# Stages one and four of a Fourier mixing in 64 x 64 quarters of the array, from even and odd sums

## The chip, the cores and the metric

The kernel runs on one core of a Trainium2 chip. The metric is the device time of one launch in microseconds (us), the median of several runs. TensorE (PE) multiplies matrices, VectorE (DVE) and ScalarE (ACT) do elementwise work and copy results out of PSUM, the memory that products are written to, POOL (GpSimd) issues the indirect DMAs and some sums, and SyncE (SP) issues all other DMAs. All arrays are float32.

## The reference

Two blocks follow one another. The first filters along the sequence in the frequency domain, the second sends each token through one of eight experts.

```python
batch, seq, dim = (8, 2496, 256)
X = np.fft.rfft(x, axis=1)
y = np.fft.irfft(X * (filt_r + 1j * filt_i)[None], n=seq, axis=1)

x = y.reshape(19968, 256)                       # N, D
logits = x @ w_gate                             # D x 8
expert_idx = np.argmax(logits, axis=1)
probs = softmax(logits); gate_w = probs[np.arange(N), expert_idx]
for e in range(8):                              # tokens of expert e
    h = np.maximum(x_sorted[lo:hi] @ w1[e], 0)  # 256 x 1024
    y_sorted[lo:hi] = h @ w2[e]                 # 1024 x 256
out = gate_w[:, None] * y_sorted[inv_perm]
```

## The kernel before

*The transform.* The sequence length is 2496 = 39 x 64. By the Chinese remainder theorem a token has two indices: q modulo 39 (`N1`) and t modulo 64 (`N2`). Each batch goes through four stages of products. Stage one (`stage_a`) is a real transform along q: 39 reals become 20 cosine and 20 sine sums. Three values of t (`NB`) share one product, with a block-diagonal table `tas` of 117 x 120. Stage two (`stage_b`, table `tbs`) is the complex transform along t, and the filter `ht` is multiplied in on VectorE. Stage three (`stage_c`, `tcs`) goes back along t, and stage four (`stage_d`, `tds`, 120 x 117) back along q.

The input of stage one is laid out on the host (`lay_x`) as 128 rows of 22 groups (`NG`), of which 117 rows are used; the last group has one t and not three. Stages one and four work in six chunks a batch, five of four groups and one of two (`CH`). Two groups are one product of 512 columns (2 x 256 channels), and each product gets a bank of PSUM (`bank`, seven of them) and one copy out of it (`evac`), on VectorE or ScalarE, whichever the planner holds to be free sooner. Between the stages the data go through memory and come back with another index on the rows: `zo` is stored to `zd` and loaded as z (`by_part`), `uo` is stored to `ud` and loaded as u (`columns`). All loads land in one set of seven buffers, `fin` (`NIN`). The first batch (`first_a`, `first_c`) stays on the chip.

*The routing.* Behind stage four each chunk `yo` is turned (`turn_y`; from batch 3 on in blocks of 32 on VectorE), multiplied with the gate (`block_logits`: eight products of 32 output columns each) and routed (`route`): small operations on VectorE find the expert and the place of each row, and one indirect DMA per group (`scatter`) writes the rows with their token number (`ids0`) and gate to `rowsd` in memory, in the order of the experts. From batch 3 on, all 128 rows of a group take part with a mask (`vld`).

*The experts.* Tiles of 512, 256 or 128 rows are read back (`rows_in`), multiplied with `w1` (`hidden_by_quarters`: both matrices in four blocks, seven products of blocks where the definition has eight, with sums on POOL and VectorE) and with `w2` (`result`, or, once the transform is done and its memory is free, `result_by_quarters`, again seven for eight).

*What sets the order.* A planner (`Order`) writes the order of each engine's instructions by hand while the program is built. It keeps a clock for each engine, with a price for each operation, and knows when a tile is ready. `slot(k)` lists the steps of the transform for batch k+1 (stage one), k (two and three) and k-1 (four and routing), each with a place in the slot, a load, its TensorE time and a class; steps of one class keep their order. The main loop takes the first step or expert product that is ready within 0.2 us and doles out products among the steps by a credit (`share`). SyncE's loads are issued by `more_loads`, stores by `flush`. Every instruction is issued by one helper, so all carry line L246 in the profile, and groups are told apart by tile names.

The lines that the change touches most are `stage_a` (530), `stage_d` (580), `columns` (473), `by_part` (503), `load_z` (515), `load_u` (520), `stage_c` (565), `route` (739), `slot` (1217), the tables in `dft_tables` (56) and the layout in `lay_x` (106). The core of stage one is

```python
for j in range(0, n, 2):
    p = bank()
    mm(p[:TK, :], lhsT=tas, rhs=xt[:TP, j:j + 2, :], start=True, stop=True)
    evac(zo[:, j:j + 2, :], p[:TK, :].rearrange("p (t d) -> p t d", t=2), 512)
```

Of the kernel before, what the change touches and what calls it, by code (L numbers as in the profile page):

```python
# [19 lines left out]
P = 128  # L20
S = 2496
# [13 lines left out]
TK = NB * NS  # L35
DH = D // P
# [4 lines left out]
NJ = D // CT  # L41

# [13 lines left out]
def dft_tables():  # L56
# [24 lines left out]

    ids = np.zeros((NB, N1, NG))
    valid = np.zeros((NB, N1, NG))
    for j in range(NB):
# [3 lines left out]

    by_block = np.zeros((4, CT, NG + 2))
    by_block.reshape(P, NG + 2)[:TP, :NG] = valid.reshape(TP, NG)  # L90
# [5 lines left out]
        "ta": ta.reshape(TP, TK),  # L96
        "tb": tb,
        "tc": tc,
        "td": np.pad(td.reshape(TK, TP), ((0, 0), (0, P - TP))),
        "sg": np.concatenate([sg[:, :NF // 2], sg[:, NF // 2:]]),  # L100
        "ids": ids.reshape(TP, NG),
        "valid": np.concatenate([np.pad(valid.reshape(TP, NG), ((0, P - TP), (0, 0))), by_block], axis=1),
    }


def lay_x(x):

    out = np.zeros((x.shape[0], P, NG, D), x.dtype)
    q = np.arange(N1)
    for j in range(NB):  # L110
        for i in range(len(range(j, N2, NB))):
            out[:, j * N1:(j + 1) * N1, i] = x[:, token(q, NB * i + j)]
    return out
# [11 lines left out]
class Order:  # L125
# [53 lines left out]
    def count(self, engine, op, args, named):  # L179
# [31 lines left out]
        else:  # L211
            if out is None:
                took = 0.8 if engine == "sync" else 0.02
            elif engine == "tensor":
# [3 lines left out]
                took = max(0.1, 0.00085 * n) if op == "transpose" else max(0.216, 0.00169 * n) if rows > 32 else 0.00045 * n  # L218
                took *= 2.0 if start < self.slow else 1.0
# [31 lines left out]
class Slots:  # L251
# [3 lines left out]
    def freed(self, name, tag):  # L255

        if name is None:
            return 0.0
        if tag in self.live and name in self.live[tag]():
            return 1e9  # L260
        return max(self.order.done.get(name, 0.0), self.order.used.get(name, 0.0)) + 0.1
# [32 lines left out]
def kernel(  # L294
# [12 lines left out]
    ids: bass.AP,  # L307
    valid: bass.AP,
# [25 lines left out]
    TR = E * TE  # L334

    dram = open_pool(ctx, name="dram", bufs=1, space=DRAM)
    zd = [dram.tile([N2, NS, D], F32, tag=f"z{b % 2}", name="zd") for b in range(B)]
    ud = [dram.tile([N2, NS, D], F32, tag=f"u{b % 2}", name="ud") for b in range(B)]
# [3 lines left out]
    rowsd = dram.tile([TR, DR], F32, tag="rows", name="rows")  # L342
# [18 lines left out]
    tas = cst.tile([TP, TK], F32, name="tas")  # L361
    tbs = cst.tile([P, P], F32, name="tbs")
    tcs = cst.tile([P, P], F32, name="tcs")
    tds = cst.tile([TK, P], F32, name="tds")
# [15 lines left out]
    ids0 = cst.tile([TP, NG], F32, name="ids0")  # L380
    vld = cst.tile([P, 2 * NG + 2], F32, name="vld")
# [12 lines left out]
    ps.live["bank"] = lambda: ()  # L394
# [25 lines left out]
    def load_filters(c):  # L420
        f0, n = FH[c]
        if c == 0:
            nc.sync.dma_start(out=tbs, in_=tb)
# [11 lines left out]
        if c == 0:  # L435
            nc.sync.dma_start(out=tcs, in_=tcm)

    def load_rest():
        nc.sync.dma_start(out=tds, in_=td)
# [33 lines left out]
    def columns(ap, i0, n):  # L473

        rows = ap.rearrange("t s d -> (t s) d")
        m = min(n, NG - 1 - i0)
        yield TK, slice(0, m), rows[i0 * TK:(i0 + m) * TK, :].rearrange("(i p) d -> p i d", p=TK)
        if m < n:
            yield NS, slice(m, n), rows[(NG - 1) * TK:, :].rearrange("(i p) d -> p i d", p=NS)
# [23 lines left out]
    def by_part(ap):  # L503

        return ap.rearrange("t (c f) d -> (t c) f d", c=2)

# [8 lines left out]
    def load_z(b, c):  # L515
        f0, n = FH[c]
        zi = fin(("z", b, c))
        nc.sync.dma_start(out=zi[:, :n], in_=by_part(zd[b])[:, f0:f0 + n, :])

    def load_u(b, c):  # L520
        i0, n = CH[c]
        ui = fin(("u", b, c))
        for r, m, v in columns(ud[b], i0, n):
# [5 lines left out]

    def stage_a(b, c):  # L530
        i0, n = CH[c]
        xt = ins.pop(("x", b, c))
        zo = sb.tile([TK, 4, D], F32, tag="st", name="zo", bufs=4)
        for j in range(0, n, 2):
            p = bank()
            mm(p[:TK, :], lhsT=tas, rhs=xt[:TP, j:j + 2, :], start=True, stop=True)
            evac(zo[:, j:j + 2, :], p[:TK, :].rearrange("p (t d) -> p t d", t=2), 512)
        for r, m, v in columns(zd[b], i0, n):
# [4 lines left out]
    def stage_b(b, f):  # L543
# [6 lines left out]
        mm(p, lhsT=tbs, rhs=zi[:, j:j + 2, :], start=True, stop=True)  # L550
# [14 lines left out]
    def stage_c(b, f):  # L565
# [4 lines left out]
        uo = outs["u", b]  # L570
        p = bank()
        mm(p, lhsT=tcs, rhs=ys, start=True, stop=True)
        evac(uo[:, j:j + 2, :], p.rearrange("p (i d) -> p i d", i=2), 512)
        if j == 2:
            f0 = f - 2
            move(by_part(ud[b])[:, f0:f0 + 4, :], uo)
# [3 lines left out]
    def stage_d(b, c):  # L580
# [7 lines left out]
        yo = outs["o", b, c] = sb.tile([P, 4, DR], F32, tag="y", name="yo", bufs=YB)  # L588
        for j in range(0, n, 2):
            p = bank()  # L590
            if i0 + j + 2 < NG:
                mm(p, lhsT=tds, rhs=ui[:TK, j:j + 2, :], start=True, stop=True)
# [6 lines left out]


# [12 lines left out]
    def first_a(c):  # L613
        i0, n = CH[c]
        xt = ins.pop(("x", 0, c))
        for j in range(0, n, 2):
            p = bank()[:, :4 * TK]
            for h in range(DH):
                for i in range(2):
                    mm(p[:, (2 * h + i) * TK:(2 * h + i + 1) * TK], lhsT=xt[:TP, j + i, h * P:(h + 1) * P], rhs=tas,  # L620
# [21 lines left out]
    def first_c(f):  # L642
        ys = outs.pop(("y", 0, f))
        p = bank().rearrange("p (h i t c) -> p h i t c", h=DH, c=2, i=2)
        for i in range(2):
            for h in range(DH):
                mm(p[:, h, i].rearrange("p t c -> p (t c)"), lhsT=ys[:, i, h * P:(h + 1) * P],
                   rhs=tcs, start=True, stop=True)
# [90 lines left out]
    def route(b, c0, c1):  # L739
# [63 lines left out]
        if by_blocks(b):  # L803
# [13 lines left out]
            nc.vector.tensor_copy(row.rearrange("p (c g) -> p g c", g=4), pr[:, :, 0])  # L817
# [5 lines left out]
        for i, yo in enumerate(yos):  # L823
            n = min(4, w - 4 * i)
            sh8 = (TP, n, 8)
            nc.gpsimd.tensor_scalar(
                yo.bitcast(I32)[:TP, :n, D:D + 8], in0=ids0[:, t0 + 4 * i:t0 + 4 * i + n, None].to_broadcast(sh8),
# [3 lines left out]
        for i in range(w):  # L831
            m = N1 if t0 + i == NG - 1 else TP
# [116 lines left out]
    def rows_in(i):  # L949
# [4 lines left out]
        ng = gis[i] = pools["moe"].tile([P, 4, DR - D], F32, tag="ng", name="ng", bufs=8)  # L954
# [262 lines left out]
    def slot(k):  # L1217
# [12 lines left out]
        elif k < B:  # L1230
            for f in range(0, NF + 4, 2):
                at = f / (NF + 4)
                if f < NF:
                    steps.append((at, lambda f=f: stage_b(k, f), ("z", k, f // 4) if f % 4 == 0 else None, 0.85, "b", lambda f=f: count("y") < 4 and [ins["z", k, f // 4]]))
                if f >= 4:
                    steps.append((at + 0.01, lambda f=f: stage_c(k, f - 4), None, 0.85, "c", lambda f=f: [outs["y", k, f - 4], 0.0 if f % 4 else sb.free("st") - 0.9]))
# [338 lines left out]
```

## Time and profile before

| | |
|---|---|
| median of 3 runs | 1475.87 us (1473.42 to 1477.14) |
| the profiled execution | 1478.19 us, span 1476.5 us |
| TensorE busy | 1440.1 us, 98% |
| its weight loads | 1147.0 us, 78% |
| VectorE busy | 848.7 us, 57% |
| ScalarE busy | 480.6 us, 33% |
| POOL busy | 822.0 us, 56% |
| products with `tas` (stage one, batches 1 to 7) | 154 records, 75.5 us |
| products with `tds` from memory (stage four, batches 1 to 7) | 168 records, 77.1 us |

A product in float32 shows as two records, each with its own weight load. Records overlap, so a group's busy time is what its records cover and not the sum of their durations. Idle time is put down to the instruction that ended it. The stages of the transform lie between the start and about 890 us, where the last logits are computed; the rest is expert products.

### The profile page before, as it was taken

To read this page: it belongs to the slowest core of one execution; us is meant where nothing else is said; L and a number is where in the kernel's file an instruction comes from. 1 tells how busy PE (TensorE), PEld (TensorE's weight loads), DVE (VectorE), ACT (ScalarE), POOL (GpSimd) and SP (SyncE) were. 2 spreads that over 40 slices of the span, in tenths; PEclk is the share of its full clock that TensorE was granted. 3 is DMA by queue.
4 is the path that set the end of the run, shared out by engine and by line. 5 is a ranking of instruction groups with operands and counts; after the bars stand their busy time and mean duration, and the time that the engine had idled before them with its cause. 6 is when DMAs were issued, how large, how long until landed. Compare 5 with 4: busy or idle time off the path is not lost.

```text
span 1476.5 us, 25693 instructions
## 1 busy us (share of the span) xinstructions
PE 1440.1 (98%) x7828; PEld 1147.0 (78%) x7828; DVE 848.7 (57%) x1819; ACT 480.6 (33%) x1004; POOL 822.0 (56%) x1213
## 2 busy tenths in 40 slices
PE   8998998999999999999999999999999999999998
PEld 6543656877677777776787778879999998999997
DVE  4667579235866675457665465567878775431110
ACT  4554452333332232322222232223232322223332
POOL 4434445635555654655465656858989878831111
PEclk9999999999999999999999999999999999999999
DMA  9759889795985585556544735556655425456661
GB/s 269 230 193 340 280 291 299 253 258 185 321 206 167 172 260 151 131 162 229 156 119 132 214 93 148 153 177 188 173 173 167 133 71 137 135 189 176 174 190 43
DMA packets 216383, 278.19 MB, mean 188 GB/s; under 512 B 124131, under 2 KB 163708, under 8 KB 216245
## 3 DMA queue, kind: packets, MB, share of 16 engines
q1 hardware_dynamic: 197125, 233.19, 53.2%
q0 software_dynamic: 19120, 43.33, 8.4%
q8 instruction: 66, 1.08, 0.3%
q14 instruction: 72, 0.59, 0.1%
HBM read 196.45 MB, written 80.64 MB: 188 GB/s over the span
## 4 chain that ended last, share of the span: by engine, by line
PE 85%; DVE 6%; DMA 4%; issue 3%; ACT 1%; POOL 0%; SPq 0%; DVEq 0%; POOLq 0%; ACTq 0%
PE bank L246 83%; DMA fin<-in_x_dram 2%; PE lt L246 2%; DVE hT L246 1%; DVE yw L246 1%; DVE ys L246 1%; DMA fin<-ud 1%; DMA fin<-zd 1%; DMA zd<-zo 1%; POOL out_dram L246 0%; DVE take L246 0%; ACT hT L246 0%; SPq L246 0%; DMA w1t<-in_moe_w_dram 0%; DMA xg<-rows 0%
## 5 line engine op out<-in xcount | busy, mean ns | idle before, releaser
L246 DVE TENSOR_TENSOR hT<-bank,hT 128x512 f32<-128x512 f32 (+1 forms) x504 | 301.9, 626 | 181.4 <-PE bank L246 101.2
L246 PE MATMUL bank<-w2t,hT 128*128 128x256 f32 (+1 forms) x1984 | 388.6, 350 | 1.6 <-DVE hT L246 1.6
L246 PEld LDWEIGHTS bank<-w2t,hT 128*128 128x128 f32 x1984 | 334.5, 190 | 49.9 <-issue 9.6
L246 PE MATMUL bank<-xT,w1t 128*128 128x256 f32 (+1 forms) x1728 | 314.9, 328 | 0.3 <-DVE hT L246 0.3
L246 POOL DMA_INDIRECT out_dram<-ys,ng x161 | 160.0, 994 | 252.5 <-ACT ys L246 121.5
L246 PEld LDWEIGHTS bank<-xT,w1t 128*128 128x128 f32 x1728 | 264.6, 191 | 33.1 <-issue 9.9
L246 ACT ACTIVATE hT<-hT 128x1024 f32<-128x1024 f32 (+1 forms) x144 | 135.5, 960 | 399.8 <-DVE hT L246 387.4
L246 POOL DMA_INDIRECT rows<-yo,row x176 | 181.9, 1033 | 70.8 <-POOL yo L246 31.3
L246 ACT ACTIVATE ys<-bank,ng 128x256 f32<-128x256 f32 x102 | 48.4, 475 | 287.4 <-PE bank L246 231.7
L246 PE MATMUL bank<-sums,wsum 128*128 128x256 f32 (+1 forms) x576 | 135.7, 358 | 1.5 <-DVE hT L246 1.5
L246 PE MATMUL bank<-w2s,hT 128*128 x592 | 132.9, 380 | 1.3 <-ACT hT L246 1.3
L246 POOL TENSOR_TENSOR wsum<-w1t 128x256 f32<-128x256 f32 x72 | 60.1, 835 | 114.5 <-PE bank L246 96.7
L246 PEld LDWEIGHTS bank<-w2s,hT 128*128 128x128 f32 x592 | 110.2, 190 | 15.8 <-ACT hT L246 2.0
L246 PEld LDWEIGHTS bank<-sums,wsum 128*128 128x128 f32 x576 | 100.3, 190 | 21.6 <-issue 11.3
L246 DVE STREAM_TRANSPOSE xT<-xg 128x512 f32<-128x512 f32 (+2 forms) x126 | 57.5, 494 | 57.7 <-PE bank L246 56.9
L246 PE MATMUL bank<-ys,tcs 128*128 128x512 f32 x140 | 73.8, 613 | 7.6 <-DVE yw L246 4.2
L246 DVE TENSOR_TENSOR ys<-bank,ht 128x512 f32<-128x512 f32 x80 | 54.9, 686 | 44.3 <-PE bank L246 38.0
L246 PE MATMUL bank<-fin,tds 120*128 120x512 f32 (+1 forms) x168 | 77.1, 580 | 3.1 <-DMA fin<-ud 2.6
L246 PE MATMUL bank<-fin,tas 117*120 117x512 f32 x154 | 75.5, 608 | 4.2 <-DMA fin<-in_x_dram 3.3
L246 PE MATMUL bank<-fin,tbs 128*128 128x512 f32 x140 | 72.7, 607 | 2.3 <-DMA fin<-zd 2.2
L246 ACT ACTIVATE hT<-bank 128x128 f32<-128x128 f32 (+1 forms) x191 | 57.2, 303 | 53.9 <-PE bank L246 45.3
L246 PE MATMUL bank<-xT,wsum 128*128 128x256 f32 (+1 forms) x288 | 68.8, 362 | 1.1 <-DVE yw L246 0.9
(171 smaller groups left out, 1778.9 us busy)
## 6 DMA issues: line engine op xcount, KB each, us to landing
w1t<-in_moe_w_dram SPq DMA_DIRECT2D x126, 512.0 KB
w2t<-in_moe_w_dram SPq DMA_DIRECT2D x68, 512.0 KB
fin<-in_x_dram SPq DMA_DIRECT2D x39, 512.0 KB
fin<-zd SPq DMA_DIRECT2D x35, 512.0 KB
ud<-uo SPq DMA_DIRECT2D x35, 512.0 KB
fin<-ud SPq DMA_DIRECT2D x35, 512.0 KB
zd<-zo SPq DMA_DIRECT2D x35, 480.0 KB
xg<-rows SPq DMA_DIRECT2D x112, 128.0 KB
```

What stands on the lines that cost most here:

```text
L246: return real(*args, **named)
```

## The change

From batch 4 on (`BA`) stage one, and from batch 3 on (`BD`) stage four, use that a cosine is even and a sine odd in q. The sums x[q] + x[39-q] meet only the cosines, the differences only the sines, each with 20 values of q. With three values of t that is 60 rows and 60 columns, so each product fits a 64 x 64 quarter of the array. A chunk of four groups is now four products of 64 rows, 64 columns and 512 moving columns: even and odd parts for each half of the groups. Two banks take them, so that the two halves of rows write to different banks in stage one, and the even and the odd part in stage four.

- `lay_x` puts q and 39-q into two slots of the same row; `fold_x` makes sum and difference in place, two operations on VectorE for each chunk, one chunk ahead of `stage_a`.
- `stage_d` copies out the odd bank only; `fold_y` adds it to, and subtracts it from, the even bank, two operations on VectorE. The even bank stays taken until then (`count("odd") < 2`).
- The parts lie 64 rows apart in `zd` and `ud`; a group has 128 rows. A load of z or a store of u is then two DMAs, one of 126 rows and one of two. Rows 60 to 63 of each half are unused; `stage_c` fills them in `ud` by two more DMAs a batch.
- The four tables have a second version each, loaded into the same tile during the run (`load_table`): `ta` in slot 3, `tb` and `td` in slot 4, `tc` in slot 3.
- Scatters carry 124 rows (`YR`) where they carried 117; rows with no token go to places behind the table (`waste`, `NW`), and the place is a maximum in the operation that copied it before.
- The planner has prices for these products (0.29 and 0.17 us), two classes "x" and "y" for the folds, and asks for two free banks for chunks of both stages. The buffers of `ng` are 7 and not 8, and the first large tile behind the transform goes by `result_by_quarters` only if its sums were begun.

```diff
+TH = NB * NF
+YR = 64 + TH
+BA, BD = 4, 3
+    taq = np.zeros((2, 64, 2, 64))
+    tdq = np.zeros((2, 64, 64))
+    for f in range(NF):
+        for r, (qr, j) in enumerate(half_rows()):
+            ang = w * ((qr * f) % N1) / N1
+            taq[:, r, 0, j * NF + f] = np.cos(ang)
+            tdq[0, j * NF + f, r] = (2.0 if f else 1.0) / S * np.cos(ang)
+            if f:
+                taq[:, r, 1, j * NF + f] = -np.sin(ang)
+                tdq[1, j * NF + f, r] = -2.0 / S * np.sin(ang)
...
+    def load_table(name, of, k):
+        tables[name] = cst.tile([P, P], F32, tag=name, name=name)
+        nc.sync.dma_start(out=tables[name], in_=of[k])
...
+    def by_part(rows, tile, quarters, f0, n):
+        if not quarters:
+            yield tile[:, :n], rows[:N2 * NS].rearrange("(t c f) d -> (t c) f d", c=2, f=NF)[:, f0:f0 + n, :]
+            return
+        m = 2 * (NG - 1)
+        for lo, hi, r in ((0, m * NB, NB), (m * NB, P, 1)):
+            at = rows[lo // NB * 64 + f0, :]
+            to = tile[lo:hi, :n]
+            dims = [[64 * D, (hi - lo) // r]] + ([[NF * D, r]] if r > 1 else []) + [[1, n * D]]
+            yield bass.AP(to.tensor, to.offset, [list(to.ap[0]), [1, n * D]]), bass.AP(at.tensor, at.offset, dims)
...
+    def fold_x(b, c):
+        m = CH[c][1] // 2
+        xt = ins["x", b, c][:YR]
+        even, odd = xt[:, :m], xt[:, m:2 * m]
+        nc.vector.tensor_tensor(odd, even, odd, op=ALU.subtract)
+        nc.vector.scalar_tensor_tensor(out=even, in0=even, scalar=2.0, in1=odd, op0=ALU.mult, op1=ALU.subtract)
+        folded.add((b, c))
...
+            m = n // 2
+            both = [bank()[:, :m * D].rearrange("p (t d) -> p t d", t=m) for _ in range(2)]
+            for part in range(2):
+                at = slice(64 * part, 64 * part + 64)
+                for h in range(2):
+                    k = slice(64 * h, 64 * h + TH)
+                    mm(both[h][at], lhsT=ta[k, at], rhs=xt[k, part * m:part * m + m], start=True, stop=True)
+            for h in range(2):
+                evac(zo[:, h * m:(h + 1) * m], both[h], m * D)
...
+        if b >= BD and f == 0:
+            at = ud[b][TH, :]
+            nc.sync.dma_start(out=bass.AP(at.tensor, at.offset, [[64 * D, 2 * NG - 2], [1, 4 * D]]), in_=ht[:2 * NG - 2, :4, :].rearrange("p f d -> p (f d)"))
+            nc.sync.dma_start(out=ud[b][(NG - 1) * P:, :], in_=ht[:, 0, :])
...
+        if b >= BD:
+            m = n // 2
+            both = [bank() for _ in range(2)]
+            for h in range(2):
+                for part in range(2):
+                    k = slice(64 * part, 64 * part + TH)
+                    mm(both[part][64 * h:64 * h + 64, :m * D].rearrange("p (i d) -> p i d", i=m), lhsT=tds[k, :64],
+                       rhs=ui[k, h * m:(h + 1) * m, :], start=True, stop=True)
+            evac(yo[:, m:n, :D], both[1][:, :m * D].rearrange("p (i d) -> p i d", i=m), m * D)
+            outs["odd", b, c] = both[0]
+            return
...
+    def fold_y(b, c):
+        m = CH[c][1] // 2
+        even = outs.pop(("odd", b, c))[:, :m * D].rearrange("p (i d) -> p i d", i=m)
+        yo = outs["o", b, c]
+        nc.vector.tensor_tensor(yo[:, :m, :D], even, yo[:, m:2 * m, :D], op=ALU.add)
+        nc.vector.tensor_tensor(yo[:, m:2 * m, :D], even, yo[:, m:2 * m, :D], op=ALU.subtract)
...
-        ng = gis[i] = pools["moe"].tile([P, 4, DR - D], F32, tag="ng", name="ng", bufs=8)
+        ng = gis[i] = pools["moe"].tile([P, 4, DR - D], F32, tag="ng", name="ng", bufs=7)
...
-            if late and i < LARGE:
+            if late and i < LARGE and (wide or i in made):
```

## The prediction

> **What bounds the kernel now.** I read four views in this order: the page's busy times, the table of stretches, the order of time on TensorE around one step of the transform, and the groups of VectorE with the waits of TensorE. Durations below are those of the one profiled execution: its span is 1476.5 us and its own time 1478.19 us; the median of the runs shown is 1475.87 us, 2.3 us below it, so the forecast is the median less the sum found on the profiled execution.
>
> ```profile
> span 1476.5 us, 25693 instructions
> ...
> PE 1440.1 (98%) x7828; PEld 1147.0 (78%) x7828; DVE 848.7 (57%) x1819; ACT 480.6 (33%) x1004; POOL 822.0 (56%) x1213
> ...
> PE 85%; DVE 6%; DMA 4%; issue 3%; ACT 1%; POOL 0%; SPq 0%; DVEq 0%; POOLq 0%; ACTq 0%
> ```
>
> TensorE is busy for 98% of the span and is 85% of the chain that ended last. So the end moves with the time that TensorE needs, as long as nothing else becomes late. The stretches (columns: length, then busy us and instructions of PE, PEld, DVE, ACT, POOL; then clock, DMA share, GB/s) show whether that holds where the change is, some 325 to 890 us, and what comes behind:
>
> ```profile
> 300.00:400.00 100.00, 100.00 (x483) 68.13 (x482) 60.06 (x134) 36.29 (x85) 51.07 (x83) 1.00 0.78 259
> 400.00:500.00 100.00, 98.70 (x502) 76.57 (x502) 61.53 (x123) 28.70 (x54) 55.99 (x87) 1.00 0.64 179
> 500.00:600.00 100.00, 99.29 (x442) 74.20 (x441) 66.89 (x141) 31.32 (x58) 51.52 (x82) 1.00 0.67 202
> 600.00:700.00 100.00, 97.54 (x474) 73.82 (x474) 61.97 (x121) 27.11 (x51) 55.64 (x87) 1.00 0.56 174
> 700.00:800.00 100.00, 100.00 (x511) 78.70 (x511) 63.86 (x135) 30.27 (x57) 53.65 (x83) 1.00 0.47 131
> 800.00:900.00 100.00, 97.19 (x531) 76.06 (x530) 52.68 (x126) 29.78 (x58) 62.39 (x99) 1.00 0.52 156
> 1000.00:1100.00 100.00, 100.00 (x681) 94.03 (x680) 79.16 (x110) 29.01 (x44) 87.44 (x94) 1.00 0.61 179
> ```
>
> From 300 to 900 us TensorE is at 97 to 100% at the full granted clock while VectorE is at 53 to 67% (367 us of 600) and the DMA engines at 47 to 78%. From 1000 to 1100 VectorE is at 79% and TensorE still has no gap: 79% of VectorE is not too much by itself. The third view has both kinds of product that I need (start, length, then records; a product in f32 leaves two records):
>
> ```profile
> 703.48 7.07 PE L246 MATMUL bank<-w2t,hT 128*128 128x256 f32 x32
> 710.48 0.64 PE L246 MATMUL lt<-yt,wb 128*32 128x128 f32 x16
> 711.05 3.72 PE L246 MATMUL bank<-w2t,hT 128*128 128x256 f32 x16
> ...
> 715.69 1.88 PE L246 MATMUL bank<-fin,tds 120*128 120x512 f32 x4
> 717.41 1.89 PE L246 MATMUL bank<-xT,w1t 128*128 128x256 f32 x8
> ```
>
> Two products of stage four (512 columns, whole array) take 717.41 - 715.69 = 1.72 us, 0.43 a record. The eight products with 32 output columns each start within 711.05 - 710.48 = 0.57 us. One after another, their 16 records of 128 columns would take 16 x 0.107 = 1.71 us (0.43 x 128/512 = 0.107), so they ran side by side, four at a time: 0.43 us. The remaining 0.14 us, and the 0.09 us between 703.48 + 32 x 0.2155 = 710.39 and 710.48, are the price of going into and out of the divided array: 0.23 to 0.24 us a visit.
>
> **The change, part by part.**
>
> *Products.* A chunk of four groups in stage one (batches 4 to 7) or four (batches 3 to 7) has two whole-array products, 1.72 us. It becomes four of 64 x 64 with 512 columns, each on its own quarter. If the four run side by side as the four strips did, they take 2 x 0.43 = 0.86 us. There are 4 x 5 + 5 x 5 = 45 such chunks; the nine last chunks of a batch have two groups, 0.86 us before and 0.43 after. Streaming saved: 45 x 0.86 + 9 x 0.43 = 42.6 us. In the changed order the 54 chunks stand in 46 runs (eight pairs adjoin), so 46 x 0.24 = 11.0 us of visits; nine of their borders touch the strip products, which switch anyway, about 0.1 us each back. Net 42.6 - 11.0 + 0.9 = 32.5 us. No row shows quarters (64 rows and 64 columns), so the price is bounded: four at a time saves 32.5 us; one at a time costs 45 x 1.72 + 9 x 0.86 = 85 us plus the visits, +95 us. I take four at a time: the nearest row, the strips, has it.
>
> A rule of the Trainium skill speaks against part of this. Besides the row above, in which four strips over the same 128 rows follow one another without a visible load, "TensorE: Matmul & The Clock Gate", Part 3, says that a weight load overlaps running products only when its row group differs. Two quarters here share each row group, so the second half's loads would stand bare; by that page's load time (its columns over 1.2 GHz, 64/1.2 = 53 ns, an estimate) the sum would be some 54 x 0.1 = 5 us less. I go by the row.
>
> *VectorE.* Added: 24 folds of x, two operations each in SBUF, and 30 folds of the output, two each from PSUM. The nearest rows (count, then busy us and mean ns):
>
> ```profile
> L246 DVE TENSOR_TENSOR hT<-bank,hT 128x512 f32<-128x512 f32 x392 | 257.8, 685 | 138.5 <-PE bank L246 92.6 <-ACT hT L246 30.9 <-issue 1.5
> L246 DVE SCALAR_TENSOR_TENSOR yw<-bank,ht 64x512 f32<-64x512 f32 x80 | 55.4, 693 | 1.1
> L246 DVE TENSOR_TENSOR ys<-ys,yw 128x512 f32<-128x512 f32 x64 | 46.1, 721 | 2.2
> L246 DVE TENSOR_TENSOR hT<-bank,hT 128x256 f32<-128x256 f32 x112 | 44.0, 421 | 42.9 <-ACT hT L246 29.1 <-PE bank L246 8.6
> ```
>
> x: 20 x (0.72 + 0.69) + 8 x 0.42 = 31.6 us. Output: 50 x 0.685 + 10 x 0.42 = 38.5 us. 70 us in all; the copies out of PSUM move a little between VectorE and ScalarE (9 more of stage one on VectorE, 6 fewer of stage four), +2 us, while ScalarE loses half of stage four's copies, about 25. VectorE from 300 on: (367 + 72) over 600 - 33 = 567 us, 77%, under the 79% that TensorE bore without a gap. Cover: the products of the experts' part, which the planner puts between the steps. If it is gone, TensorE waits for a bank or an hT. What TensorE waits for now:
>
> ```profile
> PE bank L246 <- DVE yw L246: 5.1, 3, 3.4
> PE bank L246 <- DVE hT L246: 3.9, 5, 1.6
> PE bank L246 <- DVE ys L246: 3.4, 3, 1.6
> PE bank L246 <- DMA fin<-in_x_dram: 3.3, 2, 2.4
> ```
>
> The three of VectorE are 12.4 us against 849 us of its work; 72 us more in proportion is 1 us, but queues grow faster than load, so I take +4 (bounds 0 and the whole 72). A fold of x also waits for its DMA at the head of VectorE's queue, where hT's additions stand behind it; TensorE waited 3.3 us for these loads in the whole run, so this sits inside the 4. The even bank is held until the fold, one or two banks of seven for about 2 us.
>
> *Tables, queues, rest.* Four tables are loaded a second time into the same tiles. Each load waits on SyncE for the last product that reads the old table, and what is queued behind it (stores, loads of z, u and weights) waits too; the first chunk of the stage then waits some 3 us for landing, which products cover. 0 to 4 x 3 us; I take 2. SyncE issues 51 more DMAs (45 two-row remainders, ten fills of unused rows, tables, less the last groups' separate ones), at some 0.4 us each 20 us over 570, on a queue that stands waiting for TensorE for 445 us of the run: nothing, bounds 0 and 5. Scatters carry 124 rows for 117; POOL is at 51 to 62% there: nothing, bounds 0 and 3. The tile `ng` has 7 buffers for 8: nothing, 0 to 2. One more tile goes through `result_by_quarters` (10 for 9): 112 records of 128 columns at 0.112 for 64 of 256 at 0.216, 12.5 for 13.8 us, -1.
>
> *Sum.* -32.5 - 1 + 4 + 2 = -27.5 us: 1478.19 becomes 1450.7, and on the median 1475.87 - 27.5 = 1448 us.
>
> **Rivals.**
> *A, as above*, 1440 to 1458: the bounds of the small terms, and the few us by which a new order changes small gaps.
> *B, VectorE or a queue takes half of it.* For it: VectorE goes from 61 to 77% where its work is chains of small routing operations and not the regular pattern of 1000 to 1100; a fold sits between the product and the transposition of the output. Against: from 300 to 900 the view of waits for that stretch has TensorE waiting 3.1 us for VectorE's ys, lt, yw and hT parts. If 15 us more of the 72 are bare, 1463; the range is 1458 to 1473.
> *C, slower: the quarters run two at a time.* The strips divide columns alone; no row divides rows. Then a chunk takes 1.72 + 0.24 against 1.72: nothing saved, 46 x 0.24 = 11 us lost, and 4 + 2 - 1 on top: 1476 + 16 = 1492. It decides below about 2.3 at a time (3.43/n + 0.24 = 1.72).
> *D, one at a time* (products do not divide in rows and columns together): 1476 + 95 + 5, about 1575. Only the absence of a row speaks for it.
>
> **How the numbers follow.** Two measurements of this kernel can be told apart from about 0.3%, 4.4 us. A 0.80, B 0.10, C 0.07, D 0.03. Faster: A and nearly all of B, 0.87; same: the slow end of B, 0.03; slower: C and D, 0.10. The likeliest is A's 1448. The range 1437 to 1463 holds A and the nearer half of B; C and D, the rest of B and a little below are left out.
>
> **What will show it.** Right: a chunk of `fin,ta` or `fin,td` with eight 64 x 64 records at about 1.1 us from its start to the next product's; streaming 0.22 us a product; VectorE at 73 to 80% from 330 to 860 us; waits of TensorE for VectorE under 20 us in all; the last logits some 45 us earlier, of which 18 are products that move behind the transform (in the changed order 597 us of products stand behind the last logits, 579 before, at the rates above). Wrong: records of one chunk starting 0.43 us apart instead of within a few ns (C, D); waits on folds (`fin`, `yo`) or on banks held for them (B); gaps of over 2 us at the four table loads. The forecast fails if the divided array does not run four quarters at once in f32, or if the wait for VectorE grows past 30 us.

## The result and the profile after

The changed kernel takes 1478.49 us (median of 22 runs, 1474.16 to 1484.97), the kernel before 1475.61 us on the same chip (22 runs): ratio 1.0014, 95% interval 1.0002 to 1.0027. That is no change by the 0.3% that the prediction set, and 30 us above its 1448.

The profiled execution has a span of 1472.7 us and a time of 1474.37 us. It lies 4 us under its median and that of before 2.6 us over its own, so the two profiles show 3.8 us the wrong way; for the size of an effect I go by medians. The page's busy times and the chain that ended last:

```profile
span 1472.7 us, 26434 instructions
...
PE 1417.1 (96%) x8100; PEld 1123.5 (76%) x8100; DVE 930.9 (63%) x1936; ACT 461.2 (31%) x986; POOL 870.4 (59%) x1219
...
PE 77%; DVE 7%; DMA 6%; issue 5%; POOL 2%; SPq 1%; ACT 1%; POOLq 0%; DVEq 0%; ACTq 0%
```

TensorE is busy for 23 us less, and its share of the chain fell from 85 to 77%. What DMA, "issue" and POOL hold of it rose from 7 to 13%. The stretches, with the columns as before:

```profile
300.00:400.00 100.00, 98.23 (x547) 70.17 (x546) 68.54 (x129) 30.84 (x72) 48.96 (x69) 1.00 0.77 241
400.00:500.00 100.00, 93.37 (x518) 62.41 (x517) 85.49 (x177) 29.27 (x64) 64.83 (x92) 0.98 0.86 234
500.00:600.00 100.00, 96.61 (x484) 72.37 (x483) 79.14 (x156) 27.78 (x53) 56.62 (x81) 0.98 0.79 224
600.00:700.00 100.00, 98.70 (x529) 74.00 (x528) 73.33 (x153) 27.04 (x51) 70.17 (x100) 1.00 0.67 192
330.00:860.00 530.00, 511.67 (x2792) 377.63 (x2790) 399.93 (x818) 148.15 (x307) 337.84 (x480) 0.99 0.70 197
```

TensorE is no longer full: 93% from 400 to 500 us, where it was 99. Yet the products themselves became as short as forecast. The order of time on TensorE (start, length):

```profile
538.71 0.59 PE L296 MATMUL bank<-ys,tc 128*128 128x512 f32 x1
539.23 1.09 PE L296 MATMUL bank<-fin,td 60*64 60x512 f32 x8
540.25 1.13 PE L296 MATMUL bank<-sums,wsum 128*128 128x256 f32 x4
```

Eight 64 x 64 records of a chunk, 1.02 us to the next product where two whole-array products took 1.72: four quarters run at a time. So the saving was made, and something gave it back. The waits of TensorE over the whole run (us in total, times, longest):

```profile
PE bank L296 <- DVE hT L296: 10.9, 8, 3.4
PE bank L296 <- DMA fin<-ud: 6.8, 4, 3.5
PE bank L296 <- DMA fin<-zd: 5.4, 3, 3.4
PE bank L296 <- DMA ta<-in_ta_dram: 4.2, 1, 4.2
PE bank L296 <- DVE ys L296: 4.1, 3, 2.2
PE bank L296 <- issue: 3.9, 1, 3.9
```

All waits together are 45.6 us where they were 29.6. Those for VectorE are 17.0 after 16.0; those for DMAs went from 8.1 to 20.2. Between 140 and 1000 us four gaps on TensorE are of 3.4 us and more (from a product's start to the next, less its streaming), where there was one. Each is paid twice, as the stretches at half clock that go with them show (length, busy us as above; the granted clock is the third number from the end):

```profile
174.08:180.90 6.82, 4.85 (x18) 1.59 (x19) 4.61 (x12) 2.15 (x4) 2.12 (x3) 0.50 0.60 205
286.72:290.13 3.41, 3.14 (x4) 1.17 (x4) 1.05 (x2) 0.00 (x0) 0.00 (x0) 0.50 1.01 284
447.14:450.56 3.42, 3.29 (x25) 1.30 (x26) 1.25 (x3) 0.76 (x2) 3.15 (x5) 0.50 1.45 178
552.96:556.37 3.41, 3.41 (x10) 2.67 (x9) 2.66 (x5) 2.15 (x4) 2.82 (x4) 0.50 1.00 257
```

At each of these gaps the clock is granted at half for 3.41 or 6.83 us. Up to the last products there are 37.5 us at half clock, 13.7 before. The books of the two profiled executions: products and the extra `result_by_quarters` tile -33.5 us (as forecast), waits 45.6 - 29.6 = +16, half clock (37.5 - 13.7) / 2 = +12: -5.5, against -3.8 measured. The clock is not an accident of these two executions: the mean granted clock of an execution is 0.985 at the median of the changed kernel's 22 and 0.993 to 0.995 in the kernel before (five sets of 16 to 35 executions), so (1 - clock) x span went from 7 to 10 us to 22.

### The profile page after: what moved, and what is told of

Its sections match the earlier page's. It is cut to its first block, busy times and chain, and to the rows that moved or that the text cites. A ratio compares the mean times of both kernels' runs of the same rounds, so it can differ in the third digit from the quotient of the medians.

```text
span 1472.7 us, 26434 instructions
## 1 busy us (share of the span) xinstructions
PE 1417.1 (96%) x8100; PEld 1123.5 (76%) x8100; DVE 930.9 (63%) x1936; ACT 461.2 (31%) x986; POOL 870.4 (59%) x1219
## 3 DMA queue, kind: packets, MB, share of 16 engines
q0 software_dynamic: 28080, 44.74, 9.9%
## 4 chain that ended last, share of the span: by engine, by line
PE 77%; DVE 7%; DMA 6%; issue 5%; POOL 2%; SPq 1%; ACT 1%; POOLq 0%; DVEq 0%; ACTq 0%
PE bank L296 76%; DVE hT L296 2%; DMA fin<-ud 2%; PE lt L296 1%; POOL rows L296 1%; DVE yw L296 1%; SPq L296 1%; DVE ys L296 1%; DMA fin<-zd 1%; DMA zd<-zo 1%; DMA ud<-uo 1%; DMA fin<-in_x_dram 1%; DMA rows<-yo,row 1%; DVE yo L296 1%; DMA ta<-in_ta_dram 1%
## 5 line engine op out<-in xcount | busy, mean ns | idle before, releaser
L296 PE MATMUL bank<-w2t,hT 128*128 128x256 f32 (+1 forms) x1984 | 381.2, 347 | 2.1 <-DVE hT L296 1.6
L296 PEld LDWEIGHTS bank<-w2t,hT 128*128 128x128 f32 x1984 | 330.3, 191 | 47.7 <-issue 3.4
L296 POOL DMA_INDIRECT rows<-yo,row x176 | 219.0, 1244 | 72.3 <-POOL yo L296 57.0
L296 ACT ACTIVATE ys<-bank,ng 128x256 f32<-128x256 f32 x88 | 41.7, 474 | 262.9 <-PE bank L296 227.8
L296 PE MATMUL bank<-fin,tb 128*128 128x512 f32 x140 | 74.5, 626 | 8.7 <-DMA fin<-zd 5.4
L296 PE MATMUL bank<-ys,tc 128*128 128x512 f32 x140 | 75.2, 623 | 4.7 <-DVE ys L296 4.1
L296 DVE TENSOR_TENSOR ys<-bank,ht 128x512 f32<-128x512 f32 x80 | 54.6, 682 | 26.7 <-PE bank L296 19.0
L296 PE MATMUL bank<-fin,ta 60*64 60x512 f32 (+2 forms) x258 | 60.1, 633 | 10.8 <-DMA ta<-in_ta_dram 4.2
L296 PE MATMUL bank<-sums,w1t 128*128 128x256 f32 (+1 forms) x288 | 67.7, 358 | 0.0
```

Source lines behind the costliest of these rows:

```text
L296: return real(*args, **named)
```

## The experiments

Ratios are to the kernel before on the same chip. Differences between two of these kernels are taken from their ratios unless medians are named; put together, the intervals of two ratios leave 0.2 to 0.35%, 3 to 5 us, on each. "Waits" are TensorE's waits from 140 to 1000 us by the profile, "half" the us of stretches at half clock that begin there. e1, e2, e9 and e11 leave sums out or move other rows, so their outputs are not the reference's.

| kernel | us | ratio, 95% | waits | half |
|---|---|---|---|---|
| before | 1475.6 | 1 | 15.0 | 3.4 |
| changed | 1478.5 | 1.0014 (1.0002 to 1.0027) | 31.9 | 20.5 |
| e1, folds short | 1475.3 | 0.9976 (0.9957 to 0.9995) | 30.6 | 20.5 |
| e2, one transfer for two | 1472.3 | 0.9966 (0.9940 to 0.9992) | 28.0 | 20.5 |
| e3, tables planned later | 1476.5 | 0.9988 (0.9969 to 1.0007) | 34.4 | 13.7 |
| e4, stage four alone | 1482.4 | 1.0025 (1.0007 to 1.0043) | 26.7 | 17.1 |
| e5, before, due from 0.22 | 1475.1 | 0.9991 (0.9977 to 1.0006) | 16.1 | 6.8 |
| e6, changed, due from 0.22 | 1478.8 | 1.0012 (0.9994 to 1.0031) | 31.9 | 27.3 |
| e7, before, reserve 50 | 1483.1 | 1.0050 (1.0032 to 1.0069) | 14.4 | 3.4 |
| e8, changed, reserve 50 | 1486.6 | 1.0064 (1.0040 to 1.0088) | 40.0 | 41.0 |
| e9, folds short, replanned | 1481.8 | 1.0035 (1.0021 to 1.0048) | 29.5 | 27.3 |
| e10, quarters twice | 1521.4 | 1.0315 (1.0294 to 1.0337) | 29.9 | 27.3 |
| e11, e9 with one transfer for two | 1474.0 | 0.9986 (0.9969 to 1.0003) | 23.7 | 23.9 |
| e12, stage one from batch 6 | 1469.8 | 0.9944 (0.9924 to 0.9965) | 26.2 | 17.1 |
| e13, scatters of 128 rows | 1468.0 | 0.9922 (0.9895 to 0.9948) | 28.4 | 20.5 |
| e14, tables early | 1480.4 | 1.0017 (0.9999 to 1.0034) | 27.0 | 34.1 |
| e15, e14 with 128 rows | 1474.4 | 0.9985 (0.9965 to 1.0004) | 24.5 | 30.7 |
| e16, tables early, batch 6, 128 rows | 1470.1 | 0.9942 (0.9920 to 0.9965) | 27.0 | 20.5 |
| e17, e12 with 128 rows | 1455.2 | 0.9862 (0.9834 to 0.9891) | 18.1 | 10.2 |
| e18, e6 with 128 rows | 1464.7 | 0.9930 (0.9910 to 0.9951) | 28.5 | 13.7 |

### One suspect at a time

*e1.* Three of the four fold operations of a chunk on 4 columns (of fold y, its first addition stays whole), with the planner counting the full ones, so that the order on TensorE stays:

```diff
-        nc.vector.tensor_tensor(odd, even, odd, op=ALU.subtract)
-        nc.vector.scalar_tensor_tensor(out=even, in0=even, scalar=2.0, in1=odd, op0=ALU.mult, op1=ALU.subtract)
+        nc.count("vector", "tensor_tensor", (odd, even, odd), {})
+        nc.count("vector", "scalar_tensor_tensor", (), dict(out=even, in0=even, in1=odd))
+        even, odd = even[:, :, :4], odd[:, :, :4]
+        nc.nc.vector.tensor_tensor(odd, even, odd, op=ALU.subtract)
+        nc.nc.vector.scalar_tensor_tensor(out=even, in0=even, scalar=2.0, in1=odd, op0=ALU.mult, op1=ALU.subtract)
...
```

> The changed kernel in its own order of instructions, with both operations of the fold of x and the second of the two of the output's fold cut to four columns a group (sums are left out, so the values are not the reference's). It takes some 50 of the 70 us of folds from VectorE and leaves every product, DMA and place in the order. Theory one (the folds take the saved time back: VectorE's queue is later, TensorE waits for hT, banks and folded x, and runs at half clock behind the longest waits): 1452 to 1462 us, the gap of 4 us at 443 gone, TensorE's slack from 150 to 1000 us down from 90 to under 70 us. Theory two (late DMAs: two-row remainders, fills, table loads, SyncE): within 5 us of the changed kernel's 1478.

*e2.* One DMA of 128 rows where the change has two, of 126 and 2 rows, for loads of z and stores of u, in the row pattern of the kernel before, and one of the two fills in one piece of 128 KB where it has 42 rows of 4 KB. What the planner counts stays:

```diff
-        for to, v in by_part(zd[b], zi, b >= BA, f0, n):
-            nc.sync.dma_start(out=to, in_=v)
...
+        (to, v), = by_part(zd[b], zi, False, f0, n)
+        nc.nc.sync.dma_start(out=to, in_=v)
...
```

> The changed kernel in its own order, but each load of z and store of u is one DMA of 128 rows in place of one of 126 and one of two, in the row pattern of the kernel before, and the fill of unused rows is one of 128 KB in place of 42 x 4 KB (the rows that land are other ones, so the values are not the reference's). 45 DMAs fewer on SyncE. Theory one (folds): within 4 us of 1478. Theory two (late DMAs): 1460 to 1470, with the waits of TensorE for fin and of SyncE for ud shorter.

*e3.* The planner is told that the second tables land 5 us later:

```diff
         nc.sync.dma_start(out=tables[name], in_=of[k])
+        if k:
+            nc.done[tables[name].name] += 5.0
```

> The changed kernel with one price changed: the planner is told that a table loaded again lands 5 us later than it thought, so that the first product with it is put further back and other products go ahead of it. Theory one (folds): within 4 us of 1478, the gap at 171 us gone and nothing else. Theory three (waits at the changes of stage, of which the table's 4.2 us wait at 171 us with some 4 us at half clock behind it is the largest): 5 to 9 us faster than 1478.

*e4.* `BA, BD = 8, 3`: stage four in quarters, stage one as before.

> Stage four in quarters from batch 3 on, stage one whole as before (no fold of x, no second ta and tb in use, z with one DMA). It keeps 25 of the 45 full chunks, 18 of the 32 us of saved product time, and 38 of the 70 us of folds. Theory one by the amount of folds: as before within 5 us, 1471 to 1480. If it is the fold of x in particular (it waits for a load at the head of VectorE's queue and releases stage one late): 1460 to 1468. If it is the fold of the output: 1478 to 1485.

By the ratios, e1 takes 0.38% off the changed kernel (5.6 us) and e2 0.48% (7.1 us), both in its very order on TensorE. 50 us of VectorE's work were worth 5.6 us, so the folds are not where the 30 us went; e1 is far from the 1452 to 1462 of its first theory, and e2 lies between the ranges of its two. e3, a new order, is 2 to 4 us from the changed kernel, less than the 5 to 9 of its third theory, and its waits are no smaller. e4 keeps 25 of the 45 full chunks and is slower than before: the loss is not stage one's alone, though this is a new order too.

### Is it the order?

The planner writes a new order for the changed kernel. That of before might be a lucky one. One constant moved in both kernels gives two more orders of each:

```diff
-                at = 0.8 * c / (nch + 3) - 0.1 if k == 1 else (0.35 if k == 2 else 0.2) + 0.8 * c / (nch + 3)
+                at = 0.8 * c / (nch + 3) - 0.1 if k == 1 else (0.35 if k == 2 else 0.22) + 0.8 * c / (nch + 3)
...
-    RESERVE = 60.0
+    RESERVE = 50.0
```

(The first line for e5 and e6, the last for e7 and e8.)

> The kernel before with one constant of its planner moved (stage four's steps are due from 0.22 of a stage on, and not from 0.20): the same work, another order. Theory one (the saved products are lost to work on the other engines, whatever the order): within 4 us of the kernel before, 1472 to 1480. Theory two (the order of the kernel before happens to have few stalls, and any other order costs): 5 to 20 us slower than before, 1481 to 1496.

> The changed kernel with the same constant moved. Theory one: as far from its partner (the kernel before with this constant) as the change was from before, +3 us, give or take 5. Theory two: 10 to 20 us faster than its partner, since both then have an order that was not chosen.

> The kernel before with another constant moved (50 us of experts' products are held back for the end of the Fourier part, and not 60): same work, another order. Theory one: 1472 to 1480. Theory two: 1481 to 1496.

> The changed kernel with the same constant moved. Theory one: within 5 us of its partner plus 3 us. Theory two: 10 to 20 us faster than its partner.

Changed less before is +2.9, +3.6 and +3.5 us in the three orders. An order is worth up to 8 us by itself (e7, which lies in theory two's range and not in theory one's), but the change costs the same in each within the noise, and the waits stand apart: 14.4 to 16.1 us in the orders of before, 31.9 to 40.0 in those of the changed kernel. Theory two, luck, falls. The orders do not hold quite the same products: e8 has eight tiles in `result_by_quarters` where the changed kernel has ten, some 3 us by the prediction's 1.3 a tile.

### Shorter pace, or more work?

e9 is e1 with a new order for the short folds. e10 issues each quarter twice, which gives TensorE its time back and leaves all that was added:

```diff
-            for part in range(2):
+            for part in (0, 1, 0, 1):
...
-            for h in range(2):
+            for h in (0, 1, 0, 1):
```

The planner's prices for these products go to 0.245 and 0.14 us. e11 adds e2's single transfers to e9 (there in the planner's count too), and leaves TensorE's order as in e9.

> The changed kernel with the folds of x and the second addition of the fold of y on 4 of up to 512 columns, about 50 us less VectorE, and the planner counts them so and writes a new order (the output is then not the reference's; the kernel with the short folds in the old order was 3 us faster than before). Theory one (VectorE's folds make the new waits, by way of the order as well): the waits of TensorE from 140 to 1000 us fall from 32 us to 20 or less, time 1452 to 1465. Theory two (the waits come from the shorter pace of the steps: transfers and evictions that are no longer than before, but have less TensorE time to lie under): waits 28 to 40 us, time 1470 to 1480.

> The changed kernel with every product of a quarter issued twice, the second writing over the first: all that the change adds stays (folds, second transfers, wider scatters, second tables), and TensorE's time by the streamed columns goes back to that of before and 11 us over it (42.6 us more than the changed kernel). Theory one (the added work makes the waits): they stay at 32 us or more and the half clock at 20 us, time 1516 to 1524. Theory two (the pace makes them): waits 14 to 22 us and half clock 3 to 10 us, as in the three orders of the kernel before, time 1486 to 1502.

> The changed kernel with the short folds and with one transfer of 128 rows where it has two of 126 and 2, the planner counting both and writing a new order (output not the reference's). Theory one: 1448 to 1462. Theory two: 1466 to 1476, waits of TensorE from 140 to 1000 us still 25 us or more.

The pace theory, which I held to by then, falls with e10. 42.6 us of streaming more made it 42.9 us slower than the changed kernel by the medians (44.4 by the ratios; some 4 us of this may be that its order has three tiles fewer in `result_by_quarters`), and the waits and the half clock stayed (29.9 and 27.3 us; theory one had 32 and 20, the pace theory 14 to 22 and 3 to 10). A chunk of stage four in e10, now 16 records in 1.9 us:

```profile
433.57 1.95 PE L296 MATMUL bank<-fin,td 60*64 60x512 f32 x16
443.40 2.22 PE L296 MATMUL bank<-fin,td 60*64 60x512 f32 x16
```

So the added work makes the waits, whatever the pace. e9 takes the folds out of the added work and is slower than e1, with the same work left out, by 0.59%: its new order took back more than the short folds gave, and as the pace theory foretold it has 29.5 us of waits. e11 against e9 repeats e2's step in another order that both keep: 0.49%, 7.2 us; with 1474.0 us and waits of 23.7 it lies in neither theory's range as a whole. The second transfers, with their row pattern and the small fill, are worth some 7 us.

e12 has fewer quartered chunks (`BA, BD = 6, 3`):

> The changed kernel with stage one in quarters from batch 6 on, and not from batch 4 (stage four from batch 3 on, as it was): 10 full and 2 half chunks less in quarters, 10 us of TensorE not saved, 11 chunks' folds of x and second transfers not added. Theory one (the additions cost): 1468 to 1476, faster than the changed kernel. Theory two (the pace): within 5 us of it, 1474 to 1484.

By the count of chunks it saves some 10 us less on TensorE, and it is 9 us faster than the changed kernel (10 by the ratios). Theory one had said so; it is a new order as well.

### The scatters

From the trace, the scatters of batches 3 to 7 take 1.34 us each at the median, and 1.01 before. e13 sends all 128 rows instead of 124; the four more go to rows that nothing reads.

```diff
-            m, at = (TP, ids0) if b < BD else (YR, lids[:YR])
+            m, at = (TP, ids0) if b < BD else (P, lids)
...
-            m = YR if b >= BD else N1 if t0 + i == NG - 1 else TP
+            m = P if b >= BD else N1 if t0 + i == NG - 1 else TP
```

e14 loads three of the second tables when the old one is out of use: `ta` at 0.65 of slot BA - 2, `tb` at 0.9 of slot BA - 1, `td` at 0.7 of slot BD. e15 is both, e16 both with stage one from batch 6 on.

> The changed kernel, same order, with its scatters from batch 3 on of 128 rows and not of 124; the four more go to rows that nothing reads (scatters of 128 rows elsewhere in the trace take 1.00 us, those of 124 took 1.34). Theory S (the slow scatters make the gathers late, VectorE stands still at the turn of a gathered tile and all that TensorE waits for stands behind it): scatters 1.00 us, VectorE's waits for gathered rows from 7 us to under 2, TensorE's waits from 140 to 1000 us from 32 to 26 or less, time 1466 to 1473. Theory T (the reloaded tables) or M (many small causes): 1474 to 1479.

> The changed kernel with three of the four second tables loaded as soon as the last product of the old one is out (65 to 90% of the stage before, and not at the start of the next), a new order. Theory T: no TensorE wait for a table, no half clock at 174 us, 7 us gained: 1468 to 1474. Theory S or M: the waits move elsewhere, 1474 to 1482.

> Both edits together. If the two are separate causes their gains add: 1458 to 1467. If the waits only move from one place to the next (M): 1468 to 1478.

> Both edits, and stage one in quarters from batch 6 on alone (that by itself was 6.6 us faster than before). If the additions' costs add up: 1456 to 1466, faster than all kernels so far. If each new order has its own stalls: 1467 to 1476.

e13 is 13.6 us (0.92%) faster than the changed kernel, with TensorE's order the same. Page lines on the scatters (count, busy us, mean ns, idle before) and on the queue that carries them (packets, MB, share), of before, of the changed kernel, and of e13:

```profile
q0 software_dynamic: 19120, 43.33, 8.4%
...
L246 POOL DMA_INDIRECT rows<-yo,row x176 | 181.9, 1033 | 70.8 <-POOL yo L246 31.3
```

```profile
q0 software_dynamic: 28080, 44.74, 9.9%
...
L296 POOL DMA_INDIRECT rows<-yo,row x176 | 219.0, 1244 | 72.3 <-POOL yo L296 57.0
```

```profile
q0 software_dynamic: 17520, 45.06, 8.6%
...
L296 POOL DMA_INDIRECT rows<-yo,row x176 | 180.5, 1026 | 67.6 <-POOL yo L296 30.7
```

128 rows cost 0.98 to 0.99 us each and 10560 packets less over 110 scatters: 96 small packets, most of 16 bytes, hang on each scatter of 124 rows and on none of 128.

How that reaches TensorE shows at 440 us. VectorE and TensorE in the changed kernel:

```profile
440.65 1.30 DVE L296 STREAM_TRANSPOSE xT<-xg 128x512 f32<-128x512 f32 x2 [3.37 <-DMA xg<-rows]
...
444.83 1.21 DVE L296 TENSOR_TENSOR fin<-fin 124x512 f32<-124x512 f32 x1
446.07 1.09 DVE L296 SCALAR_TENSOR_TENSOR fin<-fin 124x512 f32<-124x512 f32 x1
```

```profile
440.82 2.54 PE L296 MATMUL bank<-w2t,hT 128*128 128x256 f32 x11
447.27 1.98 PE L296 MATMUL bank<-fin,ta 60*64 60x512 f32 x8 [3.91 <-issue]
```

The view puts the 3.91 us to "issue", no wait that it can show; the fold's second operation ends at 446.07 + 1.09 = 447.16, just before the chunk. The same place in e13:

```profile
440.95 1.31 DVE L296 STREAM_TRANSPOSE xT<-xg 128x512 f32<-128x512 f32 x2 [0.16 <-DMA xg<-rows]
```

```profile
436.23 10.63 PE L296 MATMUL bank<-w2t,hT 128*128 128x256 f32 x48
447.56 0.66 PE L296 MATMUL bank<-fin,ta 60*64 60x512 f32 x4 [0.71 <-ACT ys L296]
```

In the changed kernel VectorE stands 3.37 us at the turn of gathered rows (`xg`), the filter and the fold of x behind it come late, and TensorE stands 3.91 us at the chunk that needs the fold; its clock is at half from 447.14 us on. In e13 the gathered rows are there, and the gap and the half clock are gone. This pair alone does not show that the scatter closed the gap: counted by the same product, e13's TensorE was already 4 us later at 300 us, ahead of the first of these scatters (343 us), and so came later to this place. The sum of VectorE's waits for gathered rows from 140 to 1000 us goes from 7.2 to 2.9 us (0.8 before), not under the 2 that was expected, and TensorE's waits fall less than I had put down (28.4, not 26); the half clock stays at 20.5.

The two profiled executions also show only 3.8 us of the 13.6: that of e13 is the slowest of its six, that of the changed kernel the second fastest of its 22. All executions together show where much of the rest is: (1 - clock) x span is 22 us at the median of the changed kernel and 15 in e13.

The tables are not it: e14 removes the wait for `ta` and is no faster (1480.4, in the range of theories S and M). With the early tables, e15 gains 4.7 us by the scatter and stands at 1474.4, in the range of M: a third of the gain in the changed kernel's order. e16, with three edits, is where e12 was, in the range of "each new order has its own stalls". Since each of these is also a new order, two more kernels keep an order exactly and change the scatter alone: the planner counts 124 rows, the instruction sends 128.

```diff
+        rows = what.ap[0][1]
+        if key != "pad" and key >= BD:
+            nc.count("gpsimd", "indirect_dma_start", (), dict(out=rowsd, out_offset=bass.IndirectOffsetOnAxis(ap=at[:YR], axis=0), in_=what[:YR]))
-        sc = nc.gpsimd.indirect_dma_start(
+        sc = (nc.nc if key != "pad" and key >= BD else nc).gpsimd.indirect_dma_start(
```

> The kernel with stage one in quarters from batch 6 on (6.6 us faster than before with scatters of 124 rows), in exactly its order, with scatters of 128 rows. If the slow scatter costs about 10 us whatever the order: 1458 to 1464, ratio about 0.988. If what it gained in the changed kernel's order was that order's: 1467 to 1473.

> The changed kernel with stage four due from 0.22 of a stage on (2.7 us slower than before with scatters of 124 rows), in exactly its order, with scatters of 128 rows. If the slow scatter costs about 10 us whatever the order: 1466 to 1472. If it was the one order's: 1475 to 1481.

128 rows in place of 124, TensorE's order unchanged, are worth 0.92% (changed to e13), 0.82% (e12 to e17), 0.82% (e6 to e18) and 0.32% (e14 to e15): 13.6, 12.1, 12.1 and 4.7 us. e17 and e18 are even faster than their expectations had it. The scatter is a cause in every order; why it is worth less in the fourth was not tried.

The path common to the four pairs is SyncE's queue. SyncE waits until the scatters have landed before it issues the loads of gathered rows, and the loads behind these wait with them. The profiled executions show (us; the loss of clock is (1 - clock) x span at the median of all executions):

| pair | SyncE's waits for scatters, 300 to 900 us | VectorE's waits for gathered rows, 140 to 1000 us | TensorE's waits | loss of clock |
|---|---|---|---|---|
| orders of before: before, e5, e7 | 14.8, 44.3, 34.8 | 0.8, 0.0, 0.7 | 15.0, 16.1, 14.4 | 7 to 10, 9, 11 |
| changed, e13 | 75.4, 31.9 | 7.2, 2.9 | 31.9, 28.4 | 22, 15 |
| e12, e17 | 78.5, 43.5 | 1.4, 1.6 | 26.2, 18.1 | 16, 9 |
| e6, e18 | 62.0, 39.7 | 6.1, 4.4 | 31.9, 28.5 | 23, 16 |
| e14, e15 | 57.5, 29.7 | 6.7, 0.9 | 27.0, 24.5 | 25, 21 |

VectorE's waits for gathered rows do not follow the gain (none in e12 to e17, most in e14 to e15); SyncE's waits fall by 22 to 44 us in each pair. They depend on the order too (the first row; 32.0 in e10), so they can be compared within a pair alone. In three orders the gap that goes stands behind such a wait: in e12 SyncE waits 7.9 us for the scatters from 330.7 us on, issues a load of `w2t` at 345.8, and TensorE waits 4.1 us for it at 352; in e6 and e14 it waits 8.5 and 9.8 us, then stores and loads u, and TensorE waits 3.2 and 4.8 us for that at 798 and 821. None of the three gaps is in the partner with 128 rows.

e17 is the best: 1455.2 us, 1.4% faster than before. Its busy times and two stretches:

```profile
span 1454.4 us, 26282 instructions
...
PE 1416.2 (97%) x8048; PEld 1128.0 (78%) x8048; DVE 902.1 (62%) x1908; ACT 465.2 (32%) x988; POOL 831.1 (57%) x1218
```

```profile
400.00:500.00 100.00, 97.87 (x529) 73.66 (x530) 75.33 (x144) 30.29 (x60) 57.42 (x88) 0.98 0.68 190
500.00:600.00 100.00, 100.00 (x507) 74.81 (x506) 77.02 (x154) 29.10 (x53) 50.16 (x76) 1.00 0.69 204
```

VectorE is at 75 and 77% there, and TensorE at 98 and 100%: that much load on VectorE can be borne. Its mean granted clock is 0.994 at the median, that of the kernel before.

## Why the prediction was wrong

*Products*: right. Four quarters run at a time, 1.02 us to the next product for the forecast 1.1; with the 0.09 us between the product before and the chunk (538.71 to 539.23, less 0.43 of streaming) a visit costs 0.25 us for the forecast 0.24. e10 put the streaming at 42.9 us for 42.6, which is good to a few us, since its order differs. Rivals C and D fall, and so does the doubt about the second half's weight loads: the first four records of the chunk at 539.23 start 7 ns apart, row halves and all. The second four start 0.48 us after them, 0.05 more than the streaming; whether that is a bare load is not shown, and it is inside the 1.02.

*VectorE*, +4: right in size, for another reason than the load. 399.93 of 530 us from 330 to 860 are 75%, inside the 73 to 80; its work grew by 82 us, for 72. TensorE's waits for it are 17.0 us, under the 20 of the text and far from the 30 at which the forecast was to fail. Taking 50 us of folds away gave 5.6 us. Against rival B the prediction reads 3.1 us of waits for VectorE from 300 to 900 us; its four parts add up to 3.3 (1.1, 1.0, 0.9 and 0.3), and to 4.4 with those for `ls` and `oe`. No term rests on it.

*Tables*, +2: low, but not the cause. One load of four made TensorE wait, 4.2 us at 171 us, and 6.83 us at half clock came behind it, 4.2 + 3.4 = 7.6 us; the load, issued at 168.4 us, let TensorE go at 175.9, 7.5 us later, where the forecast had some 3 for landing. Loading earlier (e14) removed that and gained nothing.

*Queues*, "nothing, bounds 0 and 5": too low. The second transfers and a fill cost 7.1 and 7.2 us in two orders. I had counted SyncE's time to issue them and its idle time, and not what they do to the loads: TensorE's waits for DMAs between 140 and 1000 us are 6.3 us in e9 and 1.0 in e11, and 11.9 in the changed kernel and 7.6 in e2. Over the whole run those of e2 are no smaller (21.3 for 20.1), so this path is shown in part only.

*Scatters*, "POOL is at 51 to 62% there: nothing, bounds 0 and 3": this is the step that failed most. I priced the seven more rows by their number and covered them by POOL's idle share. The scatter's time went up by a third and its packets by 96, and it cost 4.7 to 13.6 us in four orders. POOL's share said nothing, because it is not POOL that waits: SyncE's queue waits until the scatters have landed (75.4 us from 300 to 900 us, 31.9 with 128 rows in the same order), and the loads behind it, of gathered rows, weights and u, reach TensorE late.

*The missing term*: a gap has a price of its own. The forecast added up waits and took the clock as full. 24 us more at half clock cost some 12 us, three quarters of what the waits cost; over all executions it is 12 to 15 us. The cases in the text were built on what TensorE would wait for VectorE, and rival B has a queue only in its name.

The sum closes in part. Against the forecast 30 us are missing; in the changed kernel's own order, the scatter (13.6), the second transfers (7.1) and the folds (5.6, of which 4 were in the sum) were each taken away alone, 22 us beyond the forecast's terms if they add up, give or take some 7. That these three add up was not tried (the scatter and the tables in e15 did not), nor was a kernel with the transfers mended and its result whole. About 8 us stay without a cause. Open as well: whether the longer instruction or the small packets of the 124-row scatter do the harm (e13 takes both away), whether it is the number of transfers or their row pattern that costs in the pairs, and why stage one in quarters for batches 4 and 5 is worth less than nothing even with mended scatters (e18 and e13 against e17, in different orders).

The last logits came 21 us earlier (889 to 868 us) and not 45.

## What to carry to other kernels

When a change alters the shape of a transfer, even by a few rows and on a queue that is half idle, its price is that of the new shape; bound it by the nearest row in both directions, and ask who reads the data next. A queue that waits for one transfer holds back the loads behind it: here 8 to 10 us of waiting on SyncE became a late load of something else, and each gap of 3 us and more on TensorE was paid again at half clock. Two kernels whose orders are written anew are best compared in several orders, and a suspected cost is best taken away with the order held fixed.

## What the runs showed of the hardware

- An indirect DMA of 124 rows of 1088 bytes took 1.34 us on POOL, one of 117 rows 1.006 and one of 128 rows 0.98 to 0.99 us (medians). With 124 rows the software queue carried 28080 packets, with 128 rows 17520.
- In nine profiles (three orders of before, three of the changed kernel, e10, e13, e17) all 27 gaps of 3.0 us and more on TensorE between 140 and 1000 us (from a product's start to the next, less its streaming) came with 3.41 or 6.83 us at half clock, which began between 2.5 us before and 2 us after the gap's end. Of nine gaps of 2.0 to 3.0 us six did. Four of the 36 such stretches came with no gap of 2.0 us.
- Eight 64 x 64 records in float32, two row halves by two column halves, ran four at a time, the first four starting 7 ns apart, 1.02 us to the next product against 0.86 us of streaming.
- The subtraction of a fold on 124 x 512 took 0.67 us at the best, 0.72 on the mean and up to 1.21 us in the changed kernel (the second operation 0.69, 0.73 and up to 1.10).
- One SyncE queue held 8 to 10 us at a wait for indirect DMAs to land, and the loads issued behind it left TensorE idle for 3.2 to 4.8 us (e12, e6, e14).
